# Inverted softmax sums beside the value products, value products one step later, weights prepared in every unit: an attention and two-expert kernel

## The chip, the cores and the metric

The kernel runs on one core of a Trainium2 chip. Its time is the device time of one execution in microseconds (us). TensorE (PE) multiplies matrices into PSUM, VectorE (DVE), ScalarE (ACT) and GpSimd (POOL) work on elements, and SyncE (SP) issues most transfers. Each engine carries out its own instructions strictly in the order in which they are written; semaphores tie the engines together.

## The reference

```python
scores = scale * np.matmul(q, k.transpose(0, 1, 3, 2))          # 4 x 8 heads, 576 x 576, head 64
cum = np.cumsum(np.maximum(s, 0.0), axis=-1)
bias = -(cum[:, :, :, None] - cum[:, :, None, :])
scores = np.where(causal, -1000000000.0, scores + np.minimum(bias, 0.0))
attn = np.exp(scores - np.max(scores, axis=-1, keepdims=True))
attn = attn / (np.sum(attn, axis=-1, keepdims=True) + 1e-09)
x = np.matmul(attn, v)                                           # then 2304 tokens x 512
h = np.maximum(x @ w_in, 0.0);  x = h * h @ w_out                # first expert, 2048 wide
h = np.maximum(np.maximum(x @ w1, x @ w2), x @ w3)               # second expert, 768 wide
out = h @ w_out2
```

## The kernel before

Attention works on 16 pairs of heads, and each pair in nine units (`NU`): units 0 to 7 are 128 query rows of one of the two heads (two heads by four blocks), unit 8 holds the last 64 rows of both. Units 0 to 3 are the pair's first window (`w` = 0), units 4 to 8 its second. A unit's scores (`u_s`, L508 to L518) go into one of two PSUM tiles (`ring_s`), VectorE adds the mask and finds the maximum (`u_max`, L531), ScalarE takes the exponential and its row sums (`u_exp`, L545, sums in `sm0` and `sm1`), TensorE transposes the exponentials (`u_t`, L590) into a tile of a second ring of two (`ring_t`), ScalarE copies them out (`u_et`, L617 to L622, into `et`), and TensorE multiplies them with the values (`w_pv`, L642) into another tile of that ring. VectorE copies the result into `xT` (`w_out_`, L653).

The row sums take a way of their own. `u_t` transposes them (L597) into the free end of the tile in which the exponentials of units 5 and 8 lie. `w_cp` adds 1e-9 (L556) and inverts (L558) into `rec`. `w_keep` and `w_rows` send them through DRAM to get them on all rows (`px`), and POOL multiplies `xT` with them (`w_px`, L658).

All engines' instructions are issued unit by unit. The table `ORDER` says for each operation how many units it is ahead (+) or behind (-): in step n stand in turn the maximum of unit n+1, the sums of the window's end n-3, and so on. In some steps, given by `PUMP_U`, the planner `Slots` is pumped: it prepares weights, which arrive as 64-bit words, in nine stages (`w_job`: two loads, four VectorE operations L340 to L351, an addition L355, a cast on ScalarE L360, a subtraction L363). In attention POOL does the addition and the subtraction, later VectorE. `delays` count pumps between the stages. A tile of weights goes into one of 24 slots, or, as an early tile (`t` is None), into `spare` and through DRAM (`keep`), from which POOL brings it later (L379).

The first expert goes through the token chunks in nine visits: four with the first half of the 2048 wide layer, the fifth (384 tokens) with all of it, then four with the second half. Each step is a group of 12 products with `w_in` (L672) or with `w_out` (L798, two steps behind). The tokens of a visit are split into a high and a low part (`split_x`, L665 on ScalarE, L666 on VectorE, tiles `xs`). At a visit's end VectorE and ScalarE copy the sums out (L808, L810). The second expert (L838, L879) follows.

Over the seam between attention and the first expert TensorE is given the first 24 products (`first_products`, PSUM tiles `first`), whose tokens `first_split` splits beforehand; `PRE_AT` and `PRE_N` say from which step and how many a step, `PRE_X` when the splits stand.

Of the kernel before, what the change touches and what calls it, by code (L numbers as in the profile page):

```python
# [25 lines left out]
PRE_X = 8  # L26
PRE_AT = 0
PRE_N = 3
PUMP_U = (0, 2, 3, 4, 5, 7)
# [8 lines left out]
EARLY_FROM = 80  # L38
# [6 lines left out]
ORDER = [("max", 1), ("cp", -3), ("out0", -6), ("out1", -7), ("exp", -1), ("et", -3), ("t", -2), ("s", 2), ("pv", -5), ("rows", -13),  # L45
         ("pump", 0), ("keep", -6), ("px", -19)]
# [34 lines left out]
class Slots:  # L81
# [8 lines left out]
    def __init__(self, steps, make, bring, early, room):  # L90
        self.steps = steps
        self.uses = {}
        for n, ids in enumerate(steps):
            for i in ids:
                self.uses.setdefault(i, []).append(n)
        self.make, self.bring, self.early, self.room = make, bring, early, dict(room)
        self.free = []
        self.held = {}
        self.open = []
        self.kept = set()  # L100
        self.coming = set()
        self.pos = 0
        self.clock = 0.0
        self.last = -100.0
        self.pace = PACE_ATT
        self.delays = DELAY_ATT
        self.most = ADV_ATT
        self.idle_from = None
# [55 lines left out]
    def start(self):  # L164
        for n in range(self.pos, len(self.steps)):
            for i in self.steps[n]:
                if i in self.held or i in self.coming:
                    continue
                kept = i in self.kept
                if n - self.pos > (SOON_KEPT if kept else SOON) and (kept or self.clock - self.last < self.pace):  # L170
                    return False
                if not kept and not self.can_open():
                    return False
                if not self.free and not self.evict(n):
                    return False
                self.fill(i)
                return True
        return False

    def pump(self, time):  # L180
# [7 lines left out]
        if not self.start() and self.idle_from is not None and self.pos >= self.idle_from and \  # L188
# [26 lines left out]
def kernel(  # L215
# [272 lines left out]
    wins, ends = {}, {}  # L488
    for n, (p, u) in enumerate(units):
        if u in (U0 - 1, NU - 1):  # L490
            wins[n] = (p, int(u >= U0))
        if u in (U0 + 1, NU - 1):
            ends[n] = (p, int(u == NU - 1))
# [54 lines left out]
    tr_t = {}  # L548
# [4 lines left out]
    def w_cp(p, w):  # L553
        nu = U0 + w
        sm = small.tile([NU - U0, P], F32, tag="rec", name="rec", bufs=2)
        nc.vector.tensor_scalar(out=sm[0:nu, :].rearrange("u (h c) -> u h c", c=D), in0=tr_t.pop((p, w)), scalar1=1.0e-9,  # L556
                                scalar2=None, op0=ALU.add)
        nc.vector.reciprocal(out=sm[0:nu, :], in_=sm[0:nu, :])  # L558
        rec_t[p, w] = sm
# [18 lines left out]
    def u_t(n):  # L578
# [12 lines left out]

        if n in ends:
            _, w = ends[n]
            o = tr_t[p, w] = t[0:U0 + w, :, 7 * D:8 * D]
            sm = sums.pop((p, w))
            for h in range(2):
                nc.tensor.transpose(o[:, h, :], sm[rows(h), 0:U0 + w], identF[rows(h), rows(h)])  # L597

# [44 lines left out]

    def x_of(p, w):
# [5 lines left out]
    def w_out_(p, w):  # L650
        t = pvt.pop((p, w))
        x, n = x_of(p, w)
        nc.vector.tensor_copy(x, t[:, 0, 0:n])  # L653
        ring_t.give(t)
# [8 lines left out]
    def split_x(t0, n, kk, high, low):  # L663
        src = xT[:, kk, t0:t0 + n]
        nc.scalar.copy(out=high[:, 0:n], in_=src)  # L665
        nc.vector.tensor_tensor(out=low[:, 0:n], in0=src, in1=f32(high[:, 0:n]), op=ALU.subtract)  # L666
        return high, low
# [11 lines left out]
    def first_split(kk):  # L679
        if kk < HELD_BACK:  # L680
            high, low = (slots_a[-1 - kk][:, i, :] for i in range(2))
        else:
            high, low = (hp.tile([P, S], F32R, tag=n, name=n)[:, 0:512] for n in ("xk", "xq"))
        first_x[kk] = split_x(*chunks1[0], kk, high, low)
# [5 lines left out]
    def attention():  # L690
# [5 lines left out]
        efn = dict(cp=w_cp)  # L696
        wfn = dict(pv=w_pv, out0=w_out_, out1=w_out_, keep=w_keep, rows=w_rows, px=w_px)
# [3 lines left out]
        for n in range(-span, N + span + 1):  # L701
# [10 lines left out]
            for op, d in ORDER:  # L712
# [3 lines left out]
                elif op in efn:  # L716
                    if n + d in ends:
                        efn[op](*ends[n + d])
                elif op in wfn:
                    if n + d in wins and op not in ("out1", "out0")[wins[n + d][1]]:  # L720
                        wfn[op](*wins[n + d])
                elif 0 <= n + d < N:
                    fns[op](n + d)
            if n == N:
                phQ.close()
                banks.extend(psum(ctx, "first", 2, [P, 512]))
            if PRE and n >= N - PRE_X and (n - N + PRE_X) % 2 == 0 and (n - N + PRE_X) // 2 < KD:
                first_split((n - N + PRE_X) // 2)
# [6 lines left out]
    def experts():  # L735
# [5 lines left out]
        slots.idle_from = EARLY_FROM  # L741
# [212 lines left out]
```

## Time and profile before

| what | us |
|---|---|
| median of 3 runs | 896.93 (896.42 to 897.15) |
| profiled execution | 896.98, its span 895.2 |
| TensorE busy | 855.9 (96%) |
| VectorE busy | 514.3 (57%) |
| ScalarE busy | 332.2 (37%) |
| POOL busy | 66.9 (7%) |
| attention, to the first product of an expert's own | 0 to 189.69 |
| first expert | 189.69 to 592.62 |
| second expert | 592.62 to 895.2 |

Busy shares are means over stages. A row of the profile names line, engine, operation, the tiles written and read, and behind a bar the busy time, the mean of one in ns, and the idle time just before with what ended it.

### The profile page before, as it was taken

To read this page: it belongs to the slowest core of one execution; us is meant where nothing else is said; L and a number is where in the kernel's file an instruction comes from. 1 tells how busy PE (TensorE), PEld (TensorE's weight loads), DVE (VectorE), ACT (ScalarE), POOL (GpSimd) and SP (SyncE) were. 2 spreads that over 40 slices of the span, in tenths; PEclk is the share of its full clock that TensorE was granted. 3 is DMA by queue.
4 is the path that set the end of the run, shared out by engine and by line. 5 is a ranking of instruction groups with operands and counts; after the bars stand their busy time and mean duration, and the time that the engine had idled before them with its cause. 6 is when DMAs were issued, how large, how long until landed. Compare 5 with 4: busy or idle time off the path is not lost.

```text
span 895.2 us, 14075 instructions
## 1 busy us (share of the span) xinstructions
PE 855.9 (96%) x5446; PEld 730.0 (82%) x5446; DVE 514.3 (57%) x1079; ACT 332.2 (37%) x729; POOL 66.9 (7%) x79
## 2 busy tenths in 40 slices
PE   5999888899899999998999999999999999999998
PEld 3555555577688899997998888899999999999997
DVE  6788797868886333788888777633223131312211
ACT  5788887843333223323333333311112120212111
POOL 2133333310000000000000000110000000000000
PEclk9999999999999999999999999999999999999999
DMA  4454545212321020432425355950000000000001
GB/s 144 152 151 126 177 125 166 86 57 94 125 88 47 1 83 1 142 95 94 130 69 196 116 190 184 318 151 1 13 24 1 36 1 36 1 25 12 12 24 36
DMA packets 45267, 79.00 MB, mean 88 GB/s; under 512 B 7568, under 2 KB 17360, under 8 KB 45200
## 3 DMA queue, kind: packets, MB, share of 16 engines
q1 hardware_dynamic: 42884, 69.70, 24.3%
q0 software_dynamic: 2304, 8.39, 3.1%
q8 instruction: 43, 0.70, 0.3%
q14 instruction: 24, 0.20, 0.1%
q10 hardware_dynamic: 12, 0.01, 0.0%
HBM read 60.84 MB, written 17.22 MB: 87 GB/s over the span
## 4 chain that ended last, share of the span: by engine, by line
PE 75%; DVE 14%; ACT 6%; issue 4%; DMA 1%; DVEq 0%; ACTq 0%
PE banks L838 17%; PE banks L798 16%; PE first L838 8%; PE banks L879 8%; PE first L672 8%; PE banks L672 8%; PE pairs L642 4%; PE pairs L590 3%; DVE e L531 2%; PE pair L508 2%; DVE st L351 2%; PE pairs L508 2%; DVE r L778 2%; ACT hh L780 2%; ACT et L619 2%
## 5 line engine op out<-in xcount | busy, mean ns | idle before, releaser
L798 PE MATMUL banks<-hh,sl 128*128 128x512 f32 (+1 forms) x840 | 187.1, 371 | 4.4 <-DVE pt L808 1.8
L798 PEld LDWEIGHTS banks<-hh,sl 128*128 128x128 f32 x840 | 153.9, 189 | 27.7 <-DVE pt L808 2.2
L838 PE MATMUL banks<-xs,sl 128*128 128x384 f32 x720 | 128.7, 334 | 0.0
L838 PEld LDWEIGHTS banks<-xs,sl 128*128 128x128 f32 x720 | 125.1, 188 | 0.0
L780 ACT CAST hh<-r 128x512 fp32r<-128x512 f32 (+1 forms) x80 | 46.2, 578 | 152.8 <-DVE r L778 152.8
L672 PE MATMUL banks<-xs,sl 128*128 128x512 f32 (+1 forms) x420 | 92.0, 367 | 0.0
L672 PE MATMUL first<-xs,sl 128*128 128x512 f32 (+1 forms) x396 | 87.2, 368 | 4.4 <-DVE xs L666 3.2
L545 ACT ACTIVATE e<-e,nm 128x128 f32<-128x128 f32 (+2 forms) x144 | 83.5, 582 | 11.9 <-DVE nm L531 11.5
L672 PEld LDWEIGHTS banks<-xs,sl 128*128 128x128 f32 x420 | 76.7, 188 | 9.9
L672 PEld LDWEIGHTS first<-xs,sl 128*128 128x128 f32 x396 | 72.3, 188 | 13.9 <-DVE xs L666 3.5
L781 DVE TENSOR_TENSOR hh<-r,hh 128x512 fp32r<-128x512 f32 (+1 forms) x80 | 51.1, 639 | 51.5 <-ACT hh L780 50.2
L854 DVE TENSOR_TENSOR r<-banks,r 128x384 f32<-128x384 f32 x54 | 30.1, 557 | 78.5 <-PE banks L838 78.0
L879 PE MATMUL banks<-sl,hh 128*128 128x512 f32 (+1 forms) x342 | 74.9, 378 | 0.0
L879 PEld LDWEIGHTS banks<-sl,hh 128*128 128x128 f32 x342 | 61.8, 188 | 11.8
L858 ACT CAST hh<-r 128x384 fp32r<-128x384 f32 x36 | 18.5, 513 | 138.4 <-DVE r L854 138.4
L590 PEld LDWEIGHTS pairs<-identF,e 64*128 64x128 f32 x800 | 33.4, 139 | 30.6 <-ACT et L619 23.2
L590 PE MATMUL pairs<-identF,e 64*128 64x64 f32 x800 | 41.4, 230 | 16.8 <-ACT et L619 16.5
L642 PEld LDWEIGHTS pairs<-et,xv 128*64 128x64 f32 (+1 forms) x448 | 27.8, 135 | 31.2 <-ACT e L545 8.3
L642 PE MATMUL pairs<-et,xv 128*64 128x320 f32 (+4 forms) x448 | 52.7, 367 | 0.0
L838 PE MATMUL first<-xs,sl 128*128 128x384 f32 x288 | 52.0, 335 | 0.0
L838 PEld LDWEIGHTS first<-xs,sl 128*128 128x128 f32 x288 | 50.3, 188 | 0.5
L854 DVE TENSOR_TENSOR r<-first,r 128x384 f32<-128x384 f32 x18 | 10.0, 558 | 67.3 <-PE first L838 67.3
(104 smaller groups left out, 1116.1 us busy)
## 6 DMA issues: line engine op xcount, KB each, us to landing
st<-in_w_out_dram SPq DMA_DIRECT2D x44, 256.0 KB
st<-in_w_dram SPq DMA_DIRECT2D x36, 256.0 KB
st<-in_w_in_dram SPq DMA_DIRECT2D x32, 256.0 KB
keep_w<-spare SPq DMA_DIRECT2D x10, 512.0 KB
xk<-in_kT_dram SPq DMA_DIRECT2D x16, 288.0 KB
xq<-in_qT_dram SPq DMA_DIRECT2D x16, 288.0 KB
out_dram<-ob SPq DMA_DIRECT2D x17, 256.0 KB
xv<-in_v_main_dram SPq DMA_DIRECT2D x16, 256.0 KB
```

The costliest lines, as they stand in the source:

```text
L508: nc.tensor.matmul(b[:, j, 0:w], lhsT=d["xq"][rows(j), w - P:w], rhs=d["xk"][rows(j), 0:w], start=True, stop=False)
L545: nc.scalar.activation(out=e_u[u][:, 0:w], in_=e_u[u][:, 0:w], func=ACTF.Exp, scale=-1.0, bias=st.pop(n), accum_out=sums[p, win][:, col:co ...
L590: nc.tensor.transpose(t[:, h, at * D:(at + 1) * D], e_u[v][rows(h), k * P:(k + 1) * P], identF[rows(h), rows(h)])
L642: nc.tensor.matmul(pv[rows(j), f:(W0, W1)[w]], lhsT=xv[0:kr, j, k, :], rhs=rhs, start=(k == 0), stop=(k == last))
L672: nc.tensor.matmul(hps[:, 0:n], lhsT=w[:, wp, kk * P:(kk + 1) * P], rhs=x[kk][xp][:, 0:n], start=(kk == 0 and c == 0), stop=(kk == KD - 1 ...
L780: nc.scalar.copy(out=hh[:, 0, 0:n], in_=r[:, 0:n])
L781: nc.vector.tensor_tensor(out=hh[:, 1, 0:n], in0=r[:, 0:n], in1=f32(hh[:, 0, 0:n]), op=ALU.subtract)
L798: nc.tensor.matmul(xacc[d][:, 0:n], lhsT=w[:, wp, d * P:(d + 1) * P], rhs=hh[:, xp, 0:n], start=(m == 0 and c == 0), stop=(end and c == 2))
L838: nc.tensor.matmul(pj[j][:, 0:n], lhsT=w[:, wp, kk * P:(kk + 1) * P], rhs=xs[kk][xp][:, 0:n], start=(kk == 0 and c == 0), stop=(kk == KD - ...
L854: nc.vector.tensor_tensor(out=r[:, 0:n], in0=p[:, 0:n], in1=r[:, 0:n], op=ALU.max)
L858: nc.scalar.copy(out=hh[:, 0, 0:n], in_=r[:, 0:n])
L879: nc.tensor.matmul(po[:, 0:hi - lo], lhsT=hs[ci, f][:, hp_, t * P:(t + 1) * P], rhs=w[:, wp, lo:hi], start=(c == 0), stop=(c == 3 * NF2 - 1))
```

## The change

The sums are added to and inverted where ScalarE left them (`w_rc`, 128 rows by 4 or 5 columns), three units behind the window's end. They are transposed by one instruction behind the value products, into the second bank of the value products' tile (in `w_pv`), and `w_out_` copies them into `rec` behind the values. `u_t` has no sums any more.

`ORDER` puts the second window's value products one unit later (`pv1`, -6), so that they stand in front of the scores of unit 8, and `keep` at -7. `PUMP_U` holds all nine units instead of six; `PACE_FAR` spaces the weights that are needed more than 24 steps ahead. In the first expert early tiles are made in all visits but the first, second and fifth (`EARLY_NOT_IN`), where before they were made from step 80 on. The first products begin one unit earlier with five a unit, and each first split has a place of its own, its high part one unit ahead of its low part.

In attention POOL's additions and subtractions of weights (L355, L363 before; L359, L367 now) finish 15 tiles, before 9. Tiles that go through DRAM are 24, before 16.

```diff
-PRE_X = 8
-PRE_AT = 0
-PRE_N = 3
-PUMP_U = (0, 2, 3, 4, 5, 7)
+PRE_X = (30, 21, 12, 5)
+PRE_AT = 1
+PRE_N = 5
+PUMP_U = range(9)
-EARLY_FROM = 80
+EARLY_NOT_IN = (0, 1, 4)
+FAR = 24
+PACE_FAR = 3
-ORDER = [("max", 1), ("cp", -3), ("out0", -6), ("out1", -7), ("exp", -1), ("et", -3), ("t", -2), ("s", 2), ("pv", -5), ("rows", -13),
-         ("pump", 0), ("keep", -6), ("px", -19)]
+ORDER = [("max", 1), ("out0", -6), ("out1", -7), ("rc", -3), ("exp", -1), ("et", -3), ("t", -2), ("s", 2), ("pv0", -5), ("pv1", -6), ("rows", -13),
+         ("pump", 0), ("keep", -7), ("px", -19)]
...
-                if n - self.pos > (SOON_KEPT if kept else SOON) and (kept or self.clock - self.last < self.pace):
+                pace = self.pace if n - self.pos <= FAR else max(self.pace, PACE_FAR)
+                if n - self.pos > (SOON_KEPT if kept else SOON) and (kept or self.clock - self.last < pace):
...
-    def w_cp(p, w):
-        nu = U0 + w
-        sm = small.tile([NU - U0, P], F32, tag="rec", name="rec", bufs=2)
-        nc.vector.tensor_scalar(out=sm[0:nu, :].rearrange("u (h c) -> u h c", c=D), in0=tr_t.pop((p, w)), scalar1=1.0e-9,
-                                scalar2=None, op0=ALU.add)
-        nc.vector.reciprocal(out=sm[0:nu, :], in_=sm[0:nu, :])
-        rec_t[p, w] = sm
+    def w_rc(p, w):
+        sm = sums[p, w][:, 0:U0 + w]
+        nc.vector.tensor_scalar(out=sm, in0=sm, scalar1=1.0e-9, scalar2=None, op0=ALU.add)
+        nc.vector.reciprocal(out=sm, in_=sm)
...
-        if n in ends:
-            _, w = ends[n]
-            o = tr_t[p, w] = t[0:U0 + w, :, 7 * D:8 * D]
-            sm = sums.pop((p, w))
-            for h in range(2):
-                nc.tensor.transpose(o[:, h, :], sm[rows(h), 0:U0 + w], identF[rows(h), rows(h)])
...
+        sm = sums.pop((p, w))
+        nc.tensor.transpose(t[0:U0 + w, 1, 0:P], sm[:, 0:U0 + w], identF)
...
         nc.vector.tensor_copy(x, t[:, 0, 0:n])
+
+        sm = rec_t[p, w] = small.tile([NU - U0, P], F32, tag="rec", name="rec", bufs=2)
+        nc.vector.tensor_copy(sm[0:U0 + w, :], t[0:U0 + w, 1, 0:P])
         ring_t.give(t)
```

On TensorE, in the second pair, from the last scores of units 6 and 7 (into `pairs_92`) to the first of unit 8 (into `pair_96`), before:

```order
L510 MATMUL pairs_92<-ck_145,cq_143 128x512
L642 MATMUL pairs_90<-et_633,xv 64x320 x6
L642 MATMUL pairs_90<-et_633,xv 64x192 x2
L642 MATMUL pairs_90<-et_633,xv 64x64 x2
L590 MATMUL pairs_91<-identF,e_148 128x64 x2
L590 MATMUL pairs_91<-identF,e_149 128x64 x2
L590 MATMUL pairs_91<-identF,e_148 128x64 x2
L590 MATMUL pairs_91<-identF,e_149 128x64 x2
L515 MATMUL pair_96<-xk,xq 64x512 x2
```

The same place now (`e_148` and `e_149` are the exponentials of units 2 and 3, `sm_555` the inverted sums):

```order
L512 MATMUL pairs_92<-ck_145,cq_143 128x512
L588 MATMUL pairs_91<-identF,e_148 128x64 x2
L588 MATMUL pairs_91<-identF,e_149 128x64 x2
L588 MATMUL pairs_91<-identF,e_148 128x64 x2
L588 MATMUL pairs_91<-identF,e_149 128x64 x2
L632 MATMUL pairs_90<-et_635,xv 64x320 x6
L632 MATMUL pairs_90<-et_635,xv 64x192 x2
L632 MATMUL pairs_90<-et_635,xv 64x64 x2
L635 MATMUL pairs_90<-identF,sm_555 5x128
L517 MATMUL pair_96<-xk,xq 64x512 x2
```

The transposes and the value products have changed places, and the transposed sums stand behind the products.

On VectorE, at the seam, from the last pair's sums to the first relu's square (`first`), before:

```order
L556 TENSOR_SCALAR rec<-pairs_91 4x128
L558 RECIPROCAL rec<-rec 4x128
L653 COPY xT<-pairs_90 128x256
L556 TENSOR_SCALAR rec<-pairs_90 5x128
L558 RECIPROCAL rec<-rec 5x128
L653 COPY xT<-pairs_91 128x320
L666 TENSOR_TENSOR xs<-xT,xs 128x512 x4
L778 SCALAR_TENSOR_TENSOR r<-first_2787,r 128x512
```

And now:

```order
L646 COPY xT<-pairs_90 128x256
L649 COPY rec<-pairs_90 4x128
L556 TENSOR_SCALAR sm_2745<-sm_2745 128x5
L557 RECIPROCAL sm_2745<-sm_2745 128x5
L646 COPY xT<-pairs_91 128x320
L649 COPY rec<-pairs_91 5x128
L663 TENSOR_TENSOR xs<-xT,xs 128x512 x4
L782 SCALAR_TENSOR_TENSOR r<-first_2822,r 128x512
```

`rec` is now written behind the last value copy, where before it was written in front of it. In both kernels the second of the four `xs` tiles lies in the bytes of SBUF that held `rec`, so that ScalarE's cast into it waits for the transfer out of `rec`.

On VectorE, at the end of the fifth visit, around the split of the next visit's tokens (two `xs`), before:

```order
L781 TENSOR_TENSOR hh_4620<-r_4619,hh_4620 128x384
L363 TENSOR_TENSOR sl9_76<-wa_4565,sl9_76 128x512
L348 TENSOR_SCALAR wa_4604<-st_4527 128x512
L351 SCALAR_TENSOR_TENSOR st_4527<-st_4527,wa_4604 128x512
L355 TENSOR_TENSOR wa_4604<-st_4527 128x512
L340 TENSOR_SCALAR wa_4644<-st_4568 128x512
L344 SCALAR_TENSOR_TENSOR st_4568<-st_4568,wa_4644 128x512
L666 TENSOR_TENSOR xs_4660<-xT_60,xs_4660 128x384
L666 TENSOR_TENSOR xs_4663<-xT_60,xs_4663 128x384
L778 SCALAR_TENSOR_TENSOR r_4666<-banks1_2866,r_4666 128x384
```

And now:

```order
L782 SCALAR_TENSOR_TENSOR r_4690<-first1_2823,r_4690 128x384
L785 TENSOR_TENSOR hh_4691<-r_4690,hh_4691 128x384
L782 SCALAR_TENSOR_TENSOR r_4720<-banks0_2922,r_4720 128x384
L785 TENSOR_TENSOR hh_4721<-r_4720,hh_4721 128x384
L663 TENSOR_TENSOR xs_4750<-xT_60,xs_4750 128x384
L663 TENSOR_TENSOR xs_4753<-xT_60,xs_4753 128x384
L782 SCALAR_TENSOR_TENSOR r_4756<-banks1_2923,r_4756 128x384
```

Six operations on weights in front of the split are gone from this place.

## Rows read from the trace of the kernel before

**Rows 1.** Windows by stage: start:end, length, busy of each engine (count), clock, DMA.

```profile
22.34:173.06 150.72, 135.60 (x1654) 80.39 (x1653) 123.46 (x376) 122.00 (x318) 47.41 (x45) 1.00 0.49 145
...
189.69:314.70 125.01, 121.69 (x529) 98.52 (x528) 89.82 (x151) 43.44 (x78) 0.90 (x1) 1.00 0.20 68
314.70:457.44 142.74, 137.31 (x770) 134.95 (x769) 98.37 (x180) 46.59 (x97) 0.00 (x0) 0.99 0.26 85
457.44:592.62 135.18, 135.18 (x602) 112.42 (x602) 101.74 (x171) 44.67 (x77) 8.21 (x15) 1.00 0.61 196
...
418.00:427.00 9.00, 5.38 (x20) 5.12 (x21) 8.24 (x16) 2.59 (x6) 0.00 (x0) 0.81 0.17 61
```

**Rows 2.** Groups by line, 0 to 189.69: transposes and ScalarE's copies.

```profile
L590 PE MATMUL pairs<-identF,e 64*128 64x64 f32 x800 | 41.4, 230 | 16.8 <-ACT et L619 16.5 <-ACT e L545 0.4
...
L619 ACT COPY et<-pairs 128x768 f32<-128x768 f32 (+1 forms) x32 | 28.8, 899 | 13.5 <-DVE rec L556 11.8 <-PE pairs L642 1.6
```

**Rows 3.** Order of time in one pair: start, length, engine and operation, idle before.

```profile
74.91 0.50 ACT L545 ACTIVATE e<-e,nm 128x256 f32<-128x256 f32 x1
...
75.24 2.42 PE L642 MATMUL pairs<-et,xv 128*64 128x320 f32 x20
...
80.72 0.27 DVE L556 TENSOR_SCALAR rec<-pairs 4x128 f32<-4x128 f32 x1
...
81.08 0.80 ACT L619 COPY et<-pairs 128x768 f32<-128x768 f32 x1 [0.77 <-DVE rec L556]
...
81.93 0.71 PE L590 MATMUL pairs<-identF,e 64*128 64x64 f32 x16 [0.81 <-ACT et L619]
```

**Rows 4.** Pieces of the chain that ended last: start, length, what.

```profile
83.55 0.06 PE pairs L597 x2
...
244.15 2.72 PE banks L672 x12
...
330.86 2.08 PE banks L798 x12
```

**Rows 5.** TensorE's waits from 189.69 to 250: total, times, longest.

```profile
PE banks L798 <- DVE pt L808: 1.8, 1, 1.8
PE banks L798 <- ACT sl L360: 1.2, 2, 0.6
```

**Rows 6.** TensorE's waits from 400 to 440.

```profile
PE first L672 <- DVE xs L666: 3.2, 1, 3.2
PE first L672 <- ACT xs L665: 1.2, 1, 1.2
PE banks L798 <- DVE xT L808: 0.9, 1, 0.9
```

**Rows 7.** Order of time at the seam, engine by engine.

```profile
182.62 0.94 DVE L558 RECIPROCAL rec<-rec 5x128 f32<-5x128 f32 x1
...
186.02 1.66 ACT L665 CAST xs<-xT 128x512 fp32r<-128x512 f32 x3 [2.18 <-DMA r<-rec]
...
186.82 2.35 PE L672 MATMUL first<-sl,sl 128*128 128x512 f32 x9
...
187.41 3.72 DVE L666 TENSOR_TENSOR xs<-xT,xs 128x512 fp32r<-128x512 f32 x4
...
189.69 2.88 PE L672 MATMUL banks<-xs,sl 128*128 128x512 f32 x12
...
193.17 2.79 PE L798 MATMUL banks<-hh,sl 128*128 128x512 f32 x11 [0.23 <-DVE hh L781]
```

**Rows 8.** Weight work (tile `wa`) on DVE, ACT, POOL; the bitwise step, in attention and late.

```profile
22.34:173.06 150.72, 26.26 (x40) 4.86 (x8) 21.78 (x18) 1.00 0.49 145
...
L344 DVE SCALAR_TENSOR_TENSOR st<-st,wa 128x512 uint32<-128x512 uint32 x10 | 8.3, 833 | 0.0
...
L344 DVE SCALAR_TENSOR_TENSOR st<-st,wa 128x512 uint32<-128x512 uint32 x15 | 10.4, 693 | 0.5
```

**Rows 9.** Transfers of prepared tiles back from DRAM: count, size, us to landing.

```profile
sl<-keep_w POOLq DMA_DIRECT2D x6, 512.0 KB, 5.2
```

More of the change, by code (lines that the diff above doesn't have):

```diff
@@ L107, in __init__ @@
         self.most = ADV_ATT
-        self.idle_from = None
+        self.idle = ()
     def add(self, tiles):
@@ L187, in pump @@
                 done += job.at > 2
-        if not self.start() and self.idle_from is not None and self.pos >= self.idle_from and \
+        if not self.start() and self.pos in self.idle and \
                 self.clock - self.last >= PACE_EARLY and self.can_open():
@@ L487 @@
     units = [(p, u) for p in range(NP) for u in range(NU)]
-    wins, ends = {}, {}
+    wins = {}
     for n, (p, u) in enumerate(units):
@@ L491 @@
             wins[n] = (p, int(u >= U0))
-        if u in (U0 + 1, NU - 1):
-            ends[n] = (p, int(u == NU - 1))
     st = {}
@@ L546, in u_exp @@
                              accum_out=sums[p, win][:, col:col + 1])
-    tr_t = {}
     rs_t = {}
     rec_t = {}
-    def w_cp(p, w):
-        nu = U0 + w
-        sm = small.tile([NU - U0, P], F32, tag="rec", name="rec", bufs=2)
-        nc.vector.tensor_scalar(out=sm[0:nu, :].rearrange("u (h c) -> u h c", c=D), in0=tr_t.pop((p, w)), scalar1=1.0e-9,
-                                scalar2=None, op0=ALU.add)
-        nc.vector.reciprocal(out=sm[0:nu, :], in_=sm[0:nu, :])
-        rec_t[p, w] = sm
+    def w_rc(p, w):
+        sm = sums[p, w][:, 0:U0 + w]
+        nc.vector.tensor_scalar(out=sm, in0=sm, scalar1=1.0e-9, scalar2=None, op0=ALU.add)
+        nc.vector.reciprocal(out=sm, in_=sm)
     def w_keep(p, w):
@@ L661, with high, low_of, split_x @@
     three = ((0, 0), (0, 1), (1, 0))
[L663 to L667, printed above, removed]
+    def high(t0, n, kk, hi, lo):
+        nc.scalar.copy(out=hi[:, 0:n], in_=xT[:, kk, t0:t0 + n])
+    def low_of(t0, n, kk, hi, lo):
+        nc.vector.tensor_tensor(out=lo[:, 0:n], in0=xT[:, kk, t0:t0 + n], in1=f32(hi[:, 0:n]), op=ALU.subtract)
+    def split_x(t0, n, kk, hi, lo):
+        high(t0, n, kk, hi, lo)
+        low_of(t0, n, kk, hi, lo)
+        return hi, lo
     def h_products(hps, x, n, w):
@@ L677, with first_split @@
     first_x = {}
[L679 to L684, printed above, removed]
+    def first_split(kk, low):
+        if not low:
+            if kk < HELD_BACK:
+                first_x[kk] = tuple(slots_a[-1 - kk][:, i, :] for i in range(2))
+            else:
+                first_x[kk] = tuple(hp.tile([P, S], F32R, tag=n, name=n)[:, 0:512] for n in ("xk", "xq"))
+        (high if not low else low_of)(*chunks1[0], kk, *first_x[kk])
     def first_products():
@@ L695, in attention @@
         fns = dict(s=u_s, t=u_t, max=u_max, et=u_et, exp=u_exp)
-        efn = dict(cp=w_cp)
-        wfn = dict(pv=w_pv, out0=w_out_, out1=w_out_, keep=w_keep, rows=w_rows, px=w_px)
+        wfn = dict(rc=w_rc, pv=w_pv, pv0=w_pv, pv1=w_pv, out0=w_out_, out1=w_out_, keep=w_keep, rows=w_rows, px=w_px)
         span = max(abs(d) for _, d in ORDER)
@@ L715, in attention @@
                         slots.pump(1)
-                elif op in efn:
-                    if n + d in ends:
-                        efn[op](*ends[n + d])
                 elif op in wfn:
-                    if n + d in wins and op not in ("out1", "out0")[wins[n + d][1]]:
+                    if n + d in wins and op[-1] != "10"[wins[n + d][1]]:
                         wfn[op](*wins[n + d])
@@ L723, in attention @@
                     fns[op](n + d)
-            if n == N:
+            if n == N - PRE_AT:
                 phQ.close()
                 banks.extend(psum(ctx, "first", 2, [P, 512]))
-            if PRE and n >= N - PRE_X and (n - N + PRE_X) % 2 == 0 and (n - N + PRE_X) // 2 < KD:
-                first_split((n - N + PRE_X) // 2)
+            for kk in range(KD):
+                for later in range(2):
+                    if n == N - PRE_X[kk] + later:
+                        first_split(kk, later)
             if n >= N - PRE_AT:
@@ L740, in experts @@
         adder[0] = nc.vector
-        slots.idle_from = EARLY_FROM
+        slots.idle = set(range(len(steps)))
+        for i, step in enumerate(main1):
+            if step[1] in EARLY_NOT_IN:
+                slots.idle.discard(i)
         slots.add(slots_a[-HELD_BACK:] + [sl_p.tile([P, 2, 512], F32R, name=f"slb{i}") for i in range(SLOTS_B)])
```

## The prediction

> **What bounds the kernel now.** I read the windows by stage first [rows 1]. In attention, between the first and the fifteenth large value product of a pair, TensorE works 135.60 of 150.72 us, VectorE 123.46 and ScalarE 122.00: none is full, so somebody waits in a ring. The groups by line say who [rows 2]: the transposes of L590 stood 16.5 us waiting for ScalarE's copies `et`, over sixteen pairs, which is nearly all of what TensorE loses there. The order of time in one pair says why [rows 3]: VectorE adds to the transposed sums at 80.72 (`rec`, L556), ScalarE's copy of the fifth and sixth unit waits for that until 81.08, and only then, at 81.93, can TensorE transpose the next two units into the bank. So the sums, off the value's path, gate the pair.
>
> In the first expert a group of twelve products takes 2.72 us at 512 tokens and 2.08 at 384 [rows 4]. From 189.69 to 314.70 stand 22 groups of L672 and 22 of L798: 44 x 2.72 = 119.7 of 125.01 us, 5.3 lost. From 314.70 to 457.44 stand 62 groups of 2.08 and two of 2.72, 134.4 of 142.74, 8.3 lost. From 457.44 on 48 x 2.72 + 2 x 2.08 = 134.7 of 135.18, 0.5 lost [rows 1]. The waits name the causes [rows 5, 6]: weights not yet prepared and a late VectorE copy in the first visits; in the fifth visit's end the split of the next tokens (`xs`), queued on VectorE behind weight work. The second expert has no such loss, and nothing in it is moved on TensorE.
>
> **The change, part by part.**
>
> *Inverted sums.* The two waits of VectorE work on the ring's bank go: a reciprocal of 0.94 us [rows 7] and a 0.27 us add [rows 3] per half pair become an add and a reciprocal over four or five columns, before the transpose, and one copy out of the bank beside the value's copy. No row shows an operation on so few columns: from nothing to 0.27 us each, the nearest row; I take 0.1. The copy is like the 0.27 us add, same shape and source. VectorE saves about 2 x (1.21 - 0.47) = 1.5 us a pair, which lies beside TensorE and is worth nothing itself. What counts is that `et` no longer waits for it: **-16.5 us**. Late next is TensorE itself.
>
> *The new transpose.* Before, two halves of 64 columns took a visible 0.06 us [rows 4]. Now 128 columns go through the full height: sixteen half-height ones take 0.71 [rows 3], two of them side by side, so 64 columns cost 0.09 and 128 cost 0.18. Over 32 half pairs: 32 x 0.12 = **+3.8** (from 0, if they were equal, to 32 x 0.23 = 7.4, a 128x512 product's step of 2.72 / 12).
> The Trainium skill (TensorE: Matmul & The Clock Gate, Part 4: PE-mode transpose) gives about 275 ns for a full transpose inside a kernel; by it this estimate would be 32 x 0.21 = 6.9 instead of 3.8, and the time 3.1 later. Rows of half-height transposes speak for the smaller one.
>
> *The value products one step later.* The transposes of units 2 and 3 now stand in front of them. ScalarE gets them 2.35 us earlier, and so idles less. But they now follow the last scores at once, and the exponential they need ends at 74.91 + 0.50 = 75.41 while the products began at 75.24 [rows 3], so they wait about 0.1 a pair: **+1.5** (0 to +5).
>
> *Weights prepared in every unit.* POOL's rows of the order count 15 prepared tiles in attention, before 9. A job is 26.26 / 10 = 2.63 us of VectorE, 0.61 of ScalarE and two adds of 1.21 on POOL [rows 8]. With these VectorE has 123.5 - 14 x 1.5 + 5 x 2.63 = 116 and ScalarE 122.0 + 5 x 0.61 = 125 us, TensorE 135.6 + 28 x 0.12 = 139, so TensorE is the fullest. The price is place: the new ring runs from the copy of units 4 and 5 through the exponentials to that of unit 3, the transposes, the value products and the scores of unit 8, and a cast of a weight in it delays all. Six of the fifteen stand there: 6 x 0.61 = 3.7, of which TensorE's slightly longer own round hides a little: **+3.0** (0 to 15 x 0.61 = 9.2).
> VectorE's stages run slower beside POOL's adds: 833 ns of the bitwise L344 in attention against 693 later [rows 8], some 20%. The Trainium skill (SBUF — State Buffer, SBUF: two separate sides) calls the port that both share an exclusive lock, the second blocked for the whole instruction. By it twelve more adds would cost VectorE up to 14.5 us; by the row 6 x 2.63 x 0.2 = 3. The row decides, and VectorE has room for both.
>
> *The end of attention.* All 24 first products now stand in front of the last value products, where twelve stood behind them. What follows is new. The second of the experts' `xs` tiles lies where the last inverted sums lie, and these now come out after the last value products; ScalarE's split must wait until their transfer has read them. Before, that took from 182.62 + 0.94 to 186.02, 2.46 us, hidden behind the value products and the twelve [rows 7]. Now: 0.18 for the transpose, 0.59 (186.82 to 187.41) for the copy, 0.27 for the sums, 2.46 for the transfer: 3.5; the cast 0.55, three subtractions of 0.69 to 0.93 (3.72 / 4), and 2.04 from there to the first product with `w_out` (191.13 to 193.17): 8.1 to 8.9 after the value products. Before it was 193.17 - 186.82 - 0.25 = 6.1 with 2.7 of products in it. So 8.5 + 2.7 - 6.1 = **+5.1** (2.5 if the transfer is no wait, 5.5 with the slower subtractions). After a wait of 3.2 us in the fifth visit the granted clock was 0.81 over nine us [rows 1]; here I add **+0.5** (0 to 1.5). Behind ScalarE's split stand the first relu's; nothing else waits.
>
> *The first expert.* With 15 tiles ready nothing in the first visit is made at the last moment, and the paced far jobs leave VectorE room: of 4.8 us (5.3 less the 0.5 at the seam) **-4.3**. In the fifth visit the last three tiles of products have no weight work on VectorE between them, as the order shows, so the split is prompt: **-7.8** of 8.3. The early tiles move into the third and fourth visit, where VectorE had almost none. All 24 tiles of the second expert now go through DRAM, not 16. I cost this at nothing: the first eight come into slots free since the fifth visit; if that cover is gone, one landing of 5.2 us [rows 9] stands at the seam.
>
> *The first splits*, spread over the last thirty units: nothing, within 1 us either way.
>
> Sum: -16.5 + 3.8 + 1.5 + 3.0 + 5.1 + 0.5 - 4.3 - 7.8 = -14.7, against the profiled 896.98 (the span is 895.2): **882.3 us**. The profiled execution lies 0.05 above the median of before, 896.93, so nothing is corrected.
>
> **The rivals.**
> - *Half the wait stays.* VectorE runs late by weight jobs, and its lateness reaches the transposes by the maxima and exponentials instead of the sums. For it: ScalarE would be 125 of 141 us full and works in order. Against it: VectorE would be 116 of 141 us full, and the waits of before are nearly all at `et`. -8.3 for -16.5: 890.5.
> - *All is hidden.* Casts and exponentials fall in ScalarE's pauses, and the tail's subtractions run at 0.69: 882.3 - 4.5 - 0.8 = 877.
> - *The split is late elsewhere.* Weight work in the third and fourth visit brings the loss of 7.8 back at their ends. For it: these visits had next to no weight work and now are 70 to 87% full (an estimate from the order's counts); against it: 457.44 to 592.62 had 101.74 of 135.18 us on VectorE and lost 0.5 [rows 1]. 890.1.
> - *Slower.* Attention becomes VectorE's and ScalarE's, in order: each of the six added jobs stands on the path with all its 2.63 + 0.61, 19.4 us for the 3.0: 898.7, and with POOL's adds blocking as locks 14.5 more, 913. It decides from 1.2 us of TensorE idle per job (17.7 / 15). Against it the loads above; for it nothing but the ring.
> That the sums' change does not do what it says is held out by the order: `et` there waits for TensorE alone.
>
> **How the numbers follow.** The forecast, 878 to 887, has 46 in 100; half the wait 20; all hidden 14; the late split 11; slower 7; anything between 2. A measurement can tell about 0.2% (1.8 us) from no change. All but the slower case and a mix of two rivals lie well below 895: faster 0.88, within 0.2% 0.04, slower 0.08. The range holds the cases about the forecast and the near parts of the two at 890: 873 to 892.
>
> **What would show it.** L590's wait for `et` under 4 us in all; a pair's round near 10.0 us; in the seam a ScalarE wait of 2 to 4 us on the transfer out of `rec`, seen by TensorE; no TensorE wait over 1 us at the fifth visit's end; the second expert's stage still 302 to 303 us. A TensorE wait on ScalarE's casts, or VectorE full in attention, would make it wrong.

## The result, and the profile after

The changed kernel takes 890.19 us (median of 4 runs, 888.81 to 890.74), the kernel before 897.04 beside it: a ratio of 0.9918, 95% interval 0.9898 to 0.9937, or about 6.9 us less. The forecast was 882.3, 14.7 less. So the sign and the range were right, and half of the expected gain is missing. The profiled execution took 890.74, its span is 888.9.

Windows over the same parts of the program as before: fourteen pairs of attention from one large value product to the next, to be held against [rows 1], and the first expert from its first long run of products with `w_out` to the end of the fifth visit, in the changed kernel and then in the kernel before (start:end, length, busy time of each engine with its count, granted clock, DMA).

```profile
22.28:175.25 152.97, 144.16 (x1629) 84.99 (x1625) 122.38 (x428) 126.35 (x329) 57.69 (x56) 0.98 0.53 158
199.22:451.63 252.41, 251.99 (x1283) 230.21 (x1284) 184.43 (x322) 89.72 (x172) 4.42 (x8) 1.00 0.37 119
...
193.17:457.44 264.27, 255.75 (x1284) 231.22 (x1285) 185.40 (x326) 88.64 (x173) 0.00 (x0) 0.99 0.23 76
```

The first expert did what was forecast: the same stretch takes 252.41 us in place of 264.27, and TensorE is idle for 0.42 of it in place of 8.5. Attention did not: 152.97 us for what took 150.72. TensorE's waits in attention and at the seam behind it (total, times, longest; the waits for the first transfers, much the same before and after, are left out), and its transposes, to be held against [rows 2]:

```profile
PE pairs L588 <- DVE rec L649: 3.6, 3, 2.1
PE banks L673 <- ACT xs L660: 2.1, 1, 2.1
PE pair L510 <- DVE nm L533: 1.6, 4, 0.7
PE banks L673 <- DVE xs L663: 1.2, 1, 1.2
PE pairs L510 <- DVE nm L533: 1.2, 2, 0.9
PE pairs L588 <- ACT e L547: 1.1, 5, 0.3
PE pairs L635 <- DVE sm L557: 0.5, 1, 0.5
```

```profile
L588 PE MATMUL pairs<-identF,e 64*128 64x64 f32 x800 | 43.4, 232 | 5.5 <-DVE rec L649 3.6 <-ACT e L547 1.1
```

The 16.5 us of `et` are gone, as forecast. In their place stand waits that hardly existed. In attention they come to 8.0 us, and 6.9 of them name VectorE: for maxima (`nm`), for inverted sums (`sm`), for the copies that set a bank free (`rec`). One of the two worst places, in order of time (start, length, engine):

```profile
57.97 1.27 POOL L367 TENSOR_TENSOR sl<-wa,sl 128x512 fp32r<-128x512 f32 x1 [2.33 <-ACT sl L364]
58.02 1.25 DVE L556 TENSOR_SCALAR sm<-sm 128x4 f32<-128x4 f32 x1
...
59.30 0.18 DVE L557 RECIPROCAL sm<-sm 128x4 f32<-128x4 f32 x1
59.39 1.22 DVE L348 SCALAR_TENSOR_TENSOR st<-st,wa 128x512 uint32<-128x512 uint32 x1
...
59.53 0.27 PE L635 MATMUL pairs<-identF,sm 128*4 128x128 f32 x1 [0.52 <-DVE sm L557]
...
60.53 0.75 DVE L533 CUSTOM_DVE_ANT_0 e<-pairs,bound_l 128x576 f32<-128x576 f32 x1
```

In VectorE's queue stand the add of four sums, which takes as long as GpSimd's weight subtraction beside it, then a weight operation of 1.22, and only then the maximum of the last unit; TensorE waits 0.52 for the sums and 0.90 for the maximum. In the other place a weight operation of 1.05 us and a subtraction of the first splits (L663) stand in front of the copies that set the bank free:

```profile
168.12 0.68 DVE L663 TENSOR_TENSOR sl<-xT,sl 128x512 fp32r<-128x512 f32 x1
...
168.93 1.05 DVE L352 TENSOR_SCALAR wa<-st 128x512 uint32<-128x512 uint32 x1
...
170.45 0.27 DVE L649 COPY rec<-pairs 4x128 f32<-4x128 f32 x1
...
170.87 0.79 PE L588 MATMUL pairs<-identF,e 64*128 64x64 f32 x10 [2.06 <-DVE rec L649]
```

The second price follows at once (windows as above):

```profile
56.00:60.00 4.00, 3.44 (x47) 2.03 (x45) 3.96 (x10) 2.73 (x6) 2.03 (x2) 1.00 0.29 76
60.00:64.00 4.00, 3.10 (x36) 2.06 (x32) 3.80 (x14) 2.68 (x8) 0.06 (x1) 0.69 0.56 174
64.00:68.00 4.00, 4.00 (x34) 2.24 (x32) 3.97 (x13) 3.21 (x10) 1.91 (x2) 0.88 0.45 123
...
168.00:172.00 4.00, 1.94 (x26) 1.46 (x24) 4.00 (x15) 2.59 (x8) 2.69 (x3) 0.85 0.14 37
172.00:176.00 4.00, 4.00 (x30) 2.13 (x28) 2.84 (x10) 4.00 (x12) 2.77 (x3) 0.73 0.47 110
```

The granted clock, 1.00 all through attention before, falls in these two places, after 1.42 us of waits close together and after one wait of 2.06: part of the stretch ran at 1.2 GHz instead of 2.4. VectorE is at 3.8 to 4.0 of 4.0 us in the first four of these windows. A round is the time from one pair's large value products to the next pair's: the rounds beginning at 53.07 and 161.72 take 13.3 and 13.5 us, the other twelve 10.1 to 11.3; the quiet rounds of before took 10.47.

At the seam, TensorE, then ScalarE and VectorE, to be held against [rows 7]:

```profile
190.07 0.28 PE L635 MATMUL pairs<-identF,sm 128*5 128x128 f32 x1
190.10 0.47 PE L673 MATMUL banks<-xs,sl 128*128 128x512 f32 x1
191.78 0.73 PE L673 MATMUL banks<-xs,sl 128*128 128x512 f32 x2 [1.21 <-DVE xs L663]
194.58 4.11 PE L673 MATMUL banks<-xs,sl 128*128 128x512 f32 x9 [2.06 <-ACT xs L660]
...
199.22 2.81 PE L802 MATMUL banks<-hh,sl 128*128 128x512 f32 x11 [0.30 <-DVE hh L785]
```

```profile
193.91 1.66 ACT L660 CAST xs<-xT 128x512 fp32r<-128x512 f32 x3 [8.28 <-issue]
```

The first group with `w_out` stands 8.9 us behind the value products (199.22 - 190.07 - 0.25), 6.1 before. The nine products of 4.11 us are for the most part at the lower clock; eleven of their kind take 2.8.

### The profile page after: what moved, and what is told of

It reads as the page before. It is cut to its first block, busy times and chain, and to the rows that moved or that the text cites. A ratio compares the mean times of both kernels' runs of the same rounds, so it can differ in the third digit from the quotient of the medians.

```text
span 888.9 us, 14072 instructions
## 1 busy us (share of the span) xinstructions
PE 863.4 (97%) x5414; PEld 734.6 (83%) x5414; DVE 493.3 (55%) x1100; ACT 332.3 (37%) x729; POOL 80.7 (9%) x98
## 4 chain that ended last, share of the span: by engine, by line
PE 85%; DVE 6%; ACT 4%; issue 2%; DMA 1%; SPq 1%; POOL 0%; ACTq 0%; DVEq 0%; POOLq 0%
PE banks L802 21%; PE banks L842 17%; PE banks L673 10%; PE first L673 10%; PE first L842 8%; PE banks L883 8%; PE pairs L632 4%; ACT e L547 2%; PE pairs L588 2%; DVE e L533 1%; PE pair L510 1%; PE pairs L510 1%; PE pair L517 1%; ACT et L609 1%; PE pairs L517 1%
## 5 line engine op out<-in xcount | busy, mean ns | idle before, releaser
L802 PE MATMUL banks<-hh,sl 128*128 128x512 f32 (+1 forms) x840 | 184.6, 368 | 0.7 <-DVE pt L812 0.4
L673 PE MATMUL banks<-xs,sl 128*128 128x512 f32 (+1 forms) x420 | 94.4, 372 | 3.3 <-ACT xs L660 2.1
L862 ACT CAST hh<-r 128x384 fp32r<-128x384 f32 x36 | 18.5, 514 | 138.4 <-DVE r L858 138.4
L588 PEld LDWEIGHTS pairs<-identF,e 64*128 64x128 f32 x800 | 35.5, 141 | 26.0 <-ACT e L547 13.6
L781 ACT ACTIVATE r<-first 128x512 f32<-128x512 f32 (+1 forms) x40 | 22.1, 553 | 75.7 <-PE first L673 75.7
L588 PE MATMUL pairs<-identF,e 64*128 64x64 f32 x800 | 43.4, 232 | 5.5 <-DVE rec L649 3.6
```

The lines of the kernel that those rows point to most:

```text
L588: nc.tensor.transpose(t[:, h, at * D:(at + 1) * D], e_u[v][rows(h), k * P:(k + 1) * P], identF[rows(h), rows(h)])
L673: nc.tensor.matmul(hps[:, 0:n], lhsT=w[:, wp, kk * P:(kk + 1) * P], rhs=x[kk][xp][:, 0:n], start=(kk == 0 and c == 0), stop=(kk == KD - 1 ...
L781: nc.scalar.activation(out=r[:, 0:n], in_=hps[:, 0:n], func=ACTF.Relu)
L802: nc.tensor.matmul(xacc[d][:, 0:n], lhsT=w[:, wp, d * P:(d + 1) * P], rhs=hh[:, xp, 0:n], start=(m == 0 and c == 0), stop=(end and c == 2))
L862: nc.scalar.copy(out=hh[:, 0, 0:n], in_=r[:, 0:n])
```

## The experiments

**Attention without weights.** What is the order worth by itself? In both kernels:

```diff
-PUMP_FROM = 9
+PUMP_FROM = 999
```

The changed kernel:

> The changed kernel, but no weight is prepared during attention (the first expert's weights come in after it, so only attention is read, up to about 160 us). Theory (VectorE's and POOL's weight work stands in front of the row sums and maxima, TensorE pauses, and its clock falls after two such pauses): without it every pair round is even at 10.0 to 10.2 us, none is over 10.6, and the clock is 1.00 from 20 to 150 us; the wait of the scores for the maximum in VectorE and the wait of the sums' transpose both go below 0.5 us in all. Rival one (the new order itself makes the pauses, whatever VectorE does beside): rounds of 13 us and a granted clock below 0.9 are still there. Rival two (the order is good for about 1 us a pair and the weights cost it everywhere): the even round is 9.4 us or less.

The kernel before:

> The kernel before, with no weight prepared during attention (only attention is read, up to about 160 us). Theory (the waits of about 1 us a pair for the ring's copies stand in the order of the work, not in the weights): the round stays at 10.3 to 10.5 us and TensorE still waits about 1 us a pair for these copies. Rival (the weights make these waits too): the round falls to 9.5 us, and the changed kernel's gain is only that it lives better with the weights.

The fourteen rounds of the changed kernel without weights:

```profile
22.19:160.60 138.41, 138.41 (x1628) 82.22 (x1625) 90.88 (x368) 116.31 (x312) 21.49 (x27) 1.00 0.40 119
```

The fourteen rounds of before without weights, and the transposes in the first thirteen of them:

```profile
23.59:171.84 148.25, 135.65 (x1655) 80.65 (x1653) 101.36 (x336) 116.39 (x310) 22.12 (x28) 1.00 0.37 111
```

```profile
L590 PE MATMUL pairs<-identF,e 64*128 64x64 f32 x650 | 33.6, 230 | 11.0 <-ACT et L619 11.0
```

Changed: every round 9.88 to 9.89 us, and TensorE without one idle moment, even better than the theory. Before: the even round is 10.47, with 0.85 us of waiting per pair for `et`; the fourteenth takes 11.60, with the first splits in it, which the change spreads out. So the edit of the order is worth 0.59 us a pair, and what the changed kernel shows above 138.41 is the price of the weights: 14.6 us, of which TensorE was idle for 152.97 - 144.16 = 8.8, while its own work took 144.16 - 138.41 = 5.75 longer. In the kernel before the weights, nine tiles, cost 150.72 - 148.25 = 2.5. (The whole kernels took 967.89 and 986.25 us, since the experts then wait for their weights.)

**Planner alone, and the seam mended.** The planner's new rules in the kernel before, and `rec` in a pool of its own in the changed one:

```diff
+rec_p = ctx.enter_context(tc.tile_pool(name="recs", bufs=2))
-sm = rec_t[p, w] = small.tile([NU - U0, P], F32, tag="rec", name="rec", bufs=2)
+sm = rec_t[p, w] = rec_p.tile([NU - U0, P], F32, tag="rec", name="rec")
```

> The kernel before with only the planner's new rules on when expert weights are fetched ahead (no early fetches in the first, second and fifth visit; a pace of 3 for uses more than 24 steps off); attention is as before. Theory (the first expert's stalls at its first two visits and at the end of the fifth are the planner's): 886 to 889 us, 8 to 11 us less than before, and attention ends where it did. Rival (the first visits' stalls need the more frequent weight work in attention too): 889 to 891, only the end of the fifth visit goes.

It took 885.83 us, ratio 0.9864 (0.9845 to 0.9884): 12.2 us less, more than the whole change gives, with attention as before (rounds of 10.47) and no wait over 0.6 left in the first expert. The theory holds.

> The changed kernel with the two small tiles of the inverted sums in a place of their own, which no tile of the first expert takes over, so the split of the first chunk no longer waits for the transfer that writes the last pair's sums. Theory (the seam costs about 5 us by this transfer, and 1 us more by the lower clock after it): the first value product of the first expert starts 4 to 6 us earlier than at 198.5 to 199.2, and the kernel takes 884 to 887 us. Rival (the split waits for the ring, the x columns or VectorE just as long): the start moves by less than 1 us, 889 to 891 us.

It took 887.13 us, ratio 0.9872 (0.9853 to 0.9892), against 0.9918 for the change as it is. ScalarE and TensorE at the seam:

```profile
191.74 1.66 ACT L661 CAST xs<-xT 128x512 fp32r<-128x512 f32 x3 [4.79 <-PE pairs L636]
```

```profile
193.08 2.82 PE L674 MATMUL banks<-xs,sl 128*128 128x512 f32 x11 [1.21 <-DVE xs L664]
...
196.87 2.79 PE L803 MATMUL banks<-hh,sl 128*128 128x512 f32 x11 [0.22 <-DVE hh L786]
```

The cast stands 0.4 us behind the value products' end (191.37) in place of 3.8, and the first group with `w_out` 5.25 in place of 8.9: the transfer cost 3.65 us, somewhat below the 4 to 6 expected. The 2.06 wait and the slow nine products are gone.

**The old table for the weights.**

```diff
-PUMP_U = range(9)
+PUMP_U = (0, 2, 3, 4, 5, 7)
```

> The changed kernel with the weight work's old table of units (six of nine in place of all nine). Theory (every weight stage that attention takes on costs TensorE time now that no slack of the ring covers it): the 14 rounds from 22.3 us take 147 to 150 in place of 153.0, the first expert is no slower than 1 us more, since the planner alone took its stalls away in the run with only the planner changed; 885 to 888 us. Rival (fewer stages in attention come back as stalls in the first expert): attention shorter by as much as the expert is longer, 889 to 892.

It took 879.27 us, ratio 0.9797 (0.9776 to 0.9817): 10.9 us less than the change as it is, twice the most that was expected (885 to 888).

```profile
22.20:163.00 140.80, 138.82 (x1629) 82.37 (x1625) 110.38 (x408) 121.19 (x320) 42.78 (x45) 1.00 0.52 153
```

The fourteen rounds are 12.2 us shorter, the clock 1.00. Nine tiles cost 140.80 - 138.41 = 2.4 here, no more than the 2.5 of before. Ten of the rounds are 9.89 us, three 10.4, one 10.69. In the third, which is 10.41, the cast stands in front of an exponential (start, length, engine):

```profile
50.88 0.61 ACT L364 CAST sl<-wa 128x512 fp32r<-128x512 f32 x1
...
51.39 0.51 ACT L547 ACTIVATE e<-e,nm 128x256 f32<-128x256 f32 x1
...
52.05 0.40 PE L588 MATMUL pairs<-identF,e 64*128 64x64 f32 x6 [0.52 <-ACT e L547]
```

So three of the nine casts cost 0.52 each, where the prediction gave a cast 0.61, and the others next to nothing. The first expert gives some of it back: from its first long run of products with `w_out` to the second expert it takes 389.5 us in place of 387.4, and TensorE waits 1.3 us there for weights. Both edits at once:

> Both at once: the small tiles of the inverted sums in a place of their own, and the old table of six units for the weight work. If the two costs are apart, their gains add: 881 to 885 us. If the earlier end of attention only meets the weights later, 886 to 888 us as with the tiles moved alone.

877.03 us, ratio 0.9770 (0.9747 to 0.9793). The old table brought more than assumed and the tiles somewhat less beside it, about 2.4 us.

**GpSimd's weight operations left out.**

```diff
-adder[0].tensor_tensor(out=f32(b["a"]), in0=f32(b["high"]), in1=f32(b["low"]), op=ALU.add)
+if adder[0] is nc.vector: ...
-adder[0].tensor_tensor(out=b["t"][:, 1, :], in0=f32(b["a"]), in1=f32(b["t"][:, 0, :]), op=ALU.subtract)
+if adder[0] is nc.vector: ...
+else: nc.gpsimd.memset(f32(b["t"][:, 1, :]), 0.0)
```

> The changed kernel, but during attention GpSimd's two operations per weight tile are left out (the sum of the halves is not made, the low part is filled with zeros), so the outputs of the experts are not the reference's; VectorE and ScalarE do the same weight work as before. The undisturbed round without any weights is 9.88 us, 14 of them 138.4, and the changed kernel takes 153.0 for these 14. Theory (a GpSimd operation with two inputs holds VectorE up, and a short VectorE operation beside it takes 1.2 us in place of 0.15): the rounds of 13.3 and 13.5 us go, no short operation of VectorE takes over 0.3 us, the 14 rounds take 142 to 145. Rival (VectorE's own weight work stands in front of sums and maxima, GpSimd is innocent): the long rounds stay and the 14 take 150 or more.

```profile
22.20:169.22 147.02, 140.90 (x1628) 83.31 (x1625) 117.14 (x424) 124.79 (x326) 30.21 (x42) 1.00 0.54 163
```

147.0 lies between the two theories. The long rounds shrink to 11.4 and 11.5 and the clock stays at 1.00, so GpSimd's additions and subtractions had a hand in them; but 8.6 us over 138.4 remain without them. And of the short operations on sums three still took 0.39 to 1.28 us, beside GpSimd's multiplications of `xT`, which were left in.

**The move of the value products.** The changed kernel with both parts at -5, first as it is, then with the old table:

```diff
-("pv0", -5), ("pv1", -6)
+("pv0", -5), ("pv1", -5)
```

> The changed kernel with the second part of the value products back at its old place, behind the scores of the last unit (both parts at -5). Theory (it is this move that ends the ring's waits, so without it TensorE waits again for the ring's copies): transposes wait 0.5 to 1 us a pair for the ring's copies and the even round is 10.5 us or more; 892 to 898 us. Rival (the sums' new place ends the waits and the move does nothing): rounds and time as in the changed kernel, 888 to 891.

888.53 us (one run): the theory fell, the rival holds. The quiet rounds are 9.82 to 10.34; the transposes wait 1.8 us in all for `et`, not 8 to 16.

> The changed kernel with the old table of six units for the weight work and the second part of the value products behind the last unit's scores again (-5). The same with that part in front of the scores has an even round of 9.89 us and took 879.3; before, with the sums in the ring's old places, the round is 10.47. Theory (with the weights held equal both edits of the order have a share: the move ends the wait of the last unit's transposes): even round 10.2 to 10.35 us, 884 to 887 us. Rival (the sums alone do all of it): 9.9 us, 879 to 880.

878.70 us, ratio 0.9781 (0.9756 to 0.9807), even rounds 9.83 against 9.89. The sums' new place does it without the move. And the move by itself, in the kernel before with the new planner:

> The kernel before with the planner's new rules (885.8 us alone), and of the order only the move: the second part of the value products stands in front of the last unit's scores, the sums are transposed and copied as before. Theory (each of the two edits takes a part of the 0.58 us between 10.47 and 9.89): even round 10.1 to 10.35 us, 881 to 884 us. Rival (the move is worth nothing as long as the sums' copies hold the ring's places): 10.45 us, 885 to 887.

890.82 us, ratio 0.9918 (0.9888 to 0.9949), even rounds 10.57: some 5 us slower than without the move. TensorE then waits 5.1 us for exponentials (17 times, up to 0.7), and the 15.6 for the ring's copies stay.

**Number or place of the weights?** ScalarE casts 15 weight tiles before the last exponential in the changed kernel, 9 with the old table.

```diff
-PACE_ATT = 5
+PACE_ATT = 7.5
```

> The changed kernel, weight work in all nine units of a pair as there, but a new weight only every 7.5 units in place of 5, so that attention takes on about as many weights (8 to 10 casts between 20 and 176 us) as with the old table of six units. With that table the kernel took 879.3 us. Theory A (the number of weights counts: every further weight takes VectorE time that TensorE no longer has to spare): 879 to 882 us, the 14 rounds 141 to 144. Theory B (the units count: a stage behind units 1, 6 and 8 stands in front of the maxima and sums that TensorE needs next): rounds of over 11 us stay, 884 to 889 us.

884.58 us, ratio 0.9842 (0.9815 to 0.9869). As a test of number it failed: still 14 casts, since the delays between the stages set the rate. It shows something else: with one cast fewer, 59 weight operations on VectorE in the fourteen rounds where the change has 60, and the stages at other places, the rounds take 147.0 us, 6 less than the change as it is. Of these 6 us 2.7 are idle time of TensorE and 3.2 its own work (140.92 in place of 144.16): the clock stays at 1.00, although the same two waits of 0.52 and 0.90 us stand there too, ending at 60.61 and 62.42.

```diff
-PUMP_U = range(9)
+PUMP_U = (0, 2, 3, 4, 5, 7)
-PACE_ATT = 5
+PACE_ATT = 3.33
-DELAY_ATT = (2, 6, 2, 2, 2, 2, 4, 0, 1, 1)
+DELAY_ATT = (1, 4, 1, 1, 1, 1, 3, 0, 1, 1)
```

> The changed kernel with the old table of six units, but a new weight every 3.3 of them (and shorter delays between its stages), so that attention takes on about as many weights (13 or 14 casts between 20 and 176 us) as the changed kernel. Theory A (number): 886 to 891 us, the 14 rounds 149 us or more. Theory B (units): 879 to 883 us, the 14 rounds 141 to 144.

879.39 us with 10 casts, not 13, and 142.2 for the rounds: not decisive either. The next one holds the number and keeps all nine units:

```diff
-PACE_ATT = 5
+PACE_ATT = 7.5
-DELAY_ATT = (2, 6, 2, 2, 2, 2, 4, 0, 1, 1)
+DELAY_ATT = (3, 9, 3, 3, 3, 3, 6, 0, 2, 2)
```

> The changed kernel, weight work in all nine units, the delays between a weight's stages half as long again and a new one every 7.5 units at the earliest, so that attention takes on 10 casts, as many as in the run with six units and a quicker pace, where 14 rounds took 142.2 us and the kernel 879.4. Theory A (number): 141 to 144 us for the 14 rounds, 878 to 882 us. Theory B (units): 145 us or more with rounds over 11 us, 883 to 888 us.

10 casts, and the fourteen rounds take 142.55 us: theory A. The kernel took 882.62 (880.82 to 884.94), just above the 878 to 882 of that theory, and in its first expert TensorE waits once 1.7 us for a weight that is not ready. Then one unit added to the six at a time, 11 casts each:

```diff
-PUMP_U = range(9)
+PUMP_U = (0, 1, 2, 3, 4, 5, 7)
```

> The changed kernel with the old table of six units and unit 1 added (11 casts). By number alone 14 rounds cost 0.3 to 0.4 us a cast over 138.4: 141.5 to 143 us. If unit 1 is the one whose weight stages stand in front of what TensorE needs (the maximum of unit 3 and the pair's inverted sums), the 14 rounds take 146 us or more.

and in the same way with unit 6 and with unit 8:

> The changed kernel with the old table of six units and unit 6 added (11 casts). By number alone 141.5 to 143 us for the 14 rounds. If unit 6 is the one (a stage there stands in front of the maximum of the 576 wide last unit, right behind the copy of the value products and the first inverted sums), 146 us or more.

> The changed kernel with the old table of six units and unit 8 added (11 casts). By number alone 141.5 to 143 us for the 14 rounds. If unit 8 is the one (a stage there stands in front of the next pair's maximum and of the copies that set the bank of the first value products free), 146 us or more.

879.98, 879.45 and 879.83 us (one run each); rounds 142.6, 141.4 and 141.7. None of the three units is to blame by itself. Over the 138.4 without weights:

| casts before the last exponential | 14 rounds, us over 138.4 |
|---|---|
| 9 (old table) | 2.4 |
| 10 (six units quicker; nine units slower) | 3.8; 4.1 |
| 11 (unit 6, 8 or 1 added) | 3.0; 3.3; 4.2 |
| 14 (slower pace) | 8.6 |
| 15 (the change) | 14.6 |

Up to eleven a tile costs 0.3 to 0.4 us, from fourteen on 0.6 to 1.0. Two more runs above have 15 casts: with `rec` in a place of its own 15.0 us, without the move 12.6. The kernel before, where nine tiles cost 2.5, was not run with more of them.

**The best of it together**: tiles of their own, the old table, and no move.

> The changed kernel with the inverted sums' small tiles in a place of their own, the old table of six units for the weight work, and the second part of the value products behind the last unit's scores again. With that part in front of the scores the same kernel took 877.0 us. If the move is worth nothing (as the even rounds of 9.83 without it and 9.89 with it say): 876 to 877.5 us. If it is worth 0.2 us a pair once nothing else disturbs: 879 to 881.

875.85 us, ratio 0.9753 (0.9721 to 0.9784), the fastest of all, 21 us below before. With the move the ratio was 0.9770; the intervals overlap, so the two are not told apart, though both pairs of runs and the even rounds point the same way.

## Where the prediction was right, and the step that failed

- **Inverted sums, -16.5, with the transpose and the move, +3.8 and +1.5**: together -11.2 for sixteen pairs. With the weights as before, 150.72 became 140.80 over fourteen rounds; an estimate for sixteen is 9.92 x 16 / 14 = 11.3. Right in sum, and TensorE's own 14 rounds, put at 139, are 138.4. Of the 9.9 us the order's 0.59 a pair makes 8.3; some 1.1 lie in the round with the first splits (11.60 against 10.47 without weights), which the prediction put at nothing, within 1 us. The new transpose, put at 0.18, takes 0.20 from its start to that of the next product:

```profile
34.83 0.27 PE L635 MATMUL pairs<-identF,sm 128*5 128x128 f32 x1
35.03 1.07 PE L517 MATMUL pairs<-xk,xq 64*64 64x512 f32 x4
```

  The 275 ns of the Trainium skill (TensorE: Matmul & The Clock Gate, Part 4: PE-mode transpose) agree with the length of the row, 0.27; what a row of work loses is the step, which is shorter since the next product overlaps its end. The move's +1.5 came out by luck: it was given as a wait of 0.1 a pair for the exponential, and without weights TensorE does not wait at all. The even rounds differ by 0.06, the two pairs of runs by 0.6 and 1.2 us, with overlapping intervals.
- **Weights prepared in every unit, +3.0: this step failed.** It measures 10.9 us, by the run with the old table: 12.2 over the fourteen rounds, of which the first expert gives some 2 back. Without this step the forecast is -17.7, and the old table's run took 879.27 against 896.93, which is -17.7. The prediction priced six casts on ScalarE; in the changed kernel TensorE's waits for exponentials are 1.1 us in all. VectorE it put at nothing, since with 116 of 141 us it "has room". A mean over the stage does not show a queue. VectorE was 122.38 of 152.97 us full and 4.00 of 4.00 at the longest wait; the maxima, the sums and the bank copies that TensorE needs next stood in it behind 2.5 us of weight work per tile, and 6.9 of the 8.0 us that TensorE waited in attention name it. "VectorE full in attention" was the prediction's own sign of being wrong. The rival "half the wait stays" named part of this way, VectorE's lateness by maxima and exponentials, and these are 3.9 of the 8.0 us; the largest part, 3.6, is the copies that set a bank free, and the clock is not in it, so that its 890.5 meets the measured time is in part luck. It was turned down on the mean load and on the waits of before, nearly all at `et`. That these waits had been hiding weight work is not shown: nine tiles cost as much in the old order as in the new.
- **The clock** in attention was not in the sum: two falls, 3.4 us by the windows ((0.31 + 0.12 + 0.15 + 0.27) x 4), make up most of the 5.75 by which TensorE's own work grew; the two runs with 8.6 us of price, whose clock stayed at 1.00, have the other 2.5 as well. At the seam nine products took 4.11 us; but the group with `w_out` behind them waited for VectorE's `hh`, so what the 0.5 given there was worth can't be told.
- **The seam, +5.1**: 8.9 + 2.7 - 6.1 = 5.5. Right, by its mechanism: with the tiles apart 3.65 of it go.
- **The first expert, -4.3 - 7.8 = -12.1**: from its first long run of products with `w_out` to the second expert it takes 387.4 us in place of 399.3, which is -11.9. Right. The planner's rules alone, with nine tiles, give -10.3 of it (388.9), so most of it did not need the 15 tiles that the prediction counted on; over the whole kernel they give -12.2.

With the one step corrected and the others as measured, an estimate: -11.3 + 10.9 + 5.5 - 12.2 = -7.1; measured -6.9.

GpSimd's part was weighed in the prediction. The row above shows an add of 128x4 at 1.25 us beside a GpSimd subtraction of 1.27; in the changed kernel this add takes 0.15 to 0.17 in the ten pairs where no GpSimd operation stands beside it and 0.24 to 1.25 in the other six. The Trainium skill (SBUF — State Buffer, SBUF: two separate sides) calls the shared port a lock on which the second operation blocks entirely; the trace agrees for this operation, which ends 0.03 us behind the subtraction. A long add alone costs nothing: without any weights it takes up to 0.80 us beside GpSimd's multiplications of `xT`, and TensorE is not idle once in the fourteen rounds. What the lock decided here is bounded, not settled: leaving GpSimd's adds out gave 6 us back, but so did one tile fewer at other places. Which part of the 14.6 us is the lock, which the order in VectorE's queue, stays open; so does why the price climbs so steeply between 11 and 14 tiles. Between 14 and 15 more than half of the step is the clock.

## What to carry to other kernels

When a wait goes and another engine becomes the bound, more work in the background must be priced anew: look for every instruction that stands in the queues in front of what the bound engine needs next, and do not argue from a mean load of 80%. Nor does the price grow in step with the work: here nine tiles cost 2.4 us and fifteen 14.6. A change made of several edits should be timed edit by edit: here the planner alone (-12.2) beat the whole, and one table of units took 10.9 of the gain away. What a buffer's new tenant waits for is decided by where it lies: 1 KB a partition in a place of its own was worth 2 to 4 us.

## What the runs showed of the hardware

An add on 128x4 or 128x5 elements takes 0.15 to 0.17 us on VectorE where no GpSimd operation stands beside it, a reciprocal of them 0.18 to 0.19; the prediction took 0.1. Short waits can cost twice, but need not: in the changed kernel the granted clock fell to 0.69 over four us after waits of 0.52 and 0.90 us, while the same two waits in the run with the slower pace left it at 1.00, as did a single wait of 1.59 us (the run without GpSimd's adds, at 166.40). The length of these waits alone does not tell them apart.
